# Kept first-layer products in two slots of a scratch tile, and the first pair's sums and scaled inputs one expert sooner

## The chip, the cores and the metric

The kernel runs on one core of one Trainium2 chip. The metric is device time in microseconds (us), the median of several executions. Each run lists its span (first to last instruction) and the mean granted TensorE clock; a profiled execution adds a page and a trace. Engines are written as in the profile: PE is TensorE, PEld its weight load, DVE VectorE, ACT ScalarE, POOL GpSimd, SP SyncE. A DMA is a transfer between memories that an engine's queue issues and that lands later (a store of this kernel was issued from 218.10 to 219.30 us, and what waited for it went on at 221.40). PSUM and SBUF are the two places in which this kernel has its tiles: TensorE writes its sums to PSUM tiles (`pO`, `pA`, `pV`), and the other tiles lie in SBUF.

## The reference, cut to what matters

Attention (4 batches, 8 heads, 768 positions, 64 wide; three heads causal, five with 4 sink keys and a window of 64) gives 3072 tokens of 512. A mixture of four experts follows, each with a hidden width of 1024:

```python
p = domain_probs / (domain_probs.sum(-1, keepdims=True) + 1e-09)
for e in range(E):
    h = np.maximum(x @ w1[e], 0.0)
    out += p[:, e:e + 1] * (h @ w2[e])
```

## The kernel before

The first four token tiles go through the experts in a plain way: three together, then the fourth alone. The other 20 tiles go in ten pairs. A pair's inputs are first scaled by the expert's probability. Experts 0 to 2 have a plain first layer; the last expert's first layer, and the whole second layer, are done as 2 x 2 blocks with seven products instead of eight (Winograd's form). The attention of later batches is interleaved with the pairs, so all engines run two kinds of work in one fixed order.

The first layer of the last expert uses two accumulators in PSUM, `x` and `y`, in turn. Three of its products have to be kept in SBUF until another product is added to them, and two of these are put into the output tile, which the second layer fills later:

```python
def winograd_layer1():
    s = moe.tile([P, 3, HN], FP32, name="s1", tag="sums", bufs=1)
    o = moe.tile([P, PT, DM], FP32, name="o1", tag="o", bufs=1)
    kept = [s.rearrange("p n x -> p (n x)")[:, 0 : HT * P], o[:, 0, :], o[:, 1, :]]
    ...
    def keep(n, ps):                      # ScalarE, line 1157
        nc.scalar.copy(out=kept[n], in_=ps)
    def add(n, ps, b):                    # VectorE, line 1163
        nc.vector.tensor_tensor(out=block(b), in0=ps, in1=kept[n], op=ALU.add)   # reshapes cut
        ...                               # ReLU: negative values become 0
    product(x, w1_part(0, 0), x_part(0, 0), True);  keep(0, x)      # TensorE, line 1147
    product(y, w1_part(1, 0), x_part(0, 1), True);  add(0, y, 0)
    product(x, t(1), x_sum(1), False);              keep(1, x)
    product(y, t(0), x_sum(0), True);               keep(2, y); minus(...)
    product(x, w1_part(0, 1), x_part(1, 0), False); add(2, x, 3)
    product(y, w1_part(1, 1), x_part(0, 1), False); add(1, y, 2)
    product(x, t(2), x_part(1, 1), False);          ...             # ReLU
```

At a pair's end the output tile is stored, half by half, on SyncE's queue (`store(0)`, `store(1)`). The transposes of the next group's keys and queries are DMAs on the same queue, issued after the fourth head of a group:

```python
if n == 3 and more and g > 1:
    transpose_rows(*more)        # three transposes of keys, three of queries
```

Before the first pair, while the fourth tile passes the experts, VectorE makes the weight sums `t(n)` and the scaled inputs of the first pair:

```python
for e in range(E):
    yield from plain_steps(3, 1, e, ...)      # fourth tile: layer 1, layer 2
    if e + 1 < E:
        last_weight_sum(e)
    if e + 1 < E:
        first_weight_sums()[e]()
    if e > 0:
        (lambda: scale_inputs(pairs[0], 0), lambda: scale_inputs(pairs[0], EW), scaled_sums)[e - 1]()
```

The fourth of `first_weight_sums()` comes even later, in the first pair.

The softmax here doesn't subtract the row's maximum and nothing guards it: scores larger than these inputs give would overflow.

## Time and profile before

| | before |
|---|---|
| median of the first 3 executions | 386.12 us (384.49 to 386.32) |
| profiled execution | 384.28 us, span 382.6 us |
| PE, PEld busy | 370.5, 311.5 us |
| DVE, ACT, POOL busy | 268.3, 230.3, 112.0 us |

Matmuls overlap in the pipeline (a group of eight is shown as 0.61 us at 218.69, but the next matmul starts 0.45 us later, at 219.14), so PE's busy time alone does not tell how much is left. The prediction takes the distance from each matmul's start to the next one's and subtracts the columns at 2.4 per ns; I call the remainder the excess. The trace shows that pace: eight matmuls of 128 columns take 0.45 us there, 56 ns each (32 of them, line 983, 1.79 us from 75.86 on, 56 ns each too), and eight of 512 columns 1.73 us (77.48 to 79.21), 216 ns each, so 384 more columns take 160 ns. A wait line reads: who waited, for whom, total us, times, longest us. "Idle" in a timeline's brackets is somewhat less than the excess, since the modelled end of the matmul before lies some 0.16 us after the time at which the next could have started.

### The profile page before, as it was taken

The numbers are of one execution on the slowest core, as the hardware profiler recorded it, in microseconds if no ns is written. First come the engines' busy times: TensorE is split into PE (matmuls) and PEld (weight loads), VectorE is DVE, ScalarE is ACT, GpSimd is POOL, SyncE is SP. The second block draws the span as 40 slices with busy tenths as digits, with TensorE's granted clock in tenths as the row PEclk, the third lists the DMA queues.
The fourth block names the chain that finished last, engine by engine and source line by source line (L and its number), as shares of the span: only waits on it lengthen the run. The fifth ranks groups of instructions, "written<-read, shape, count | busy, mean of one in ns | idle before, by whom it ended". The sixth has DMA issues, their size and how long they took to land.

```text
span 382.6 us, 9934 instructions
## 1 busy us (share of the span) xinstructions
PE 370.5 (97%) x4054; PEld 311.5 (81%) x4054; DVE 268.3 (70%) x590; ACT 230.3 (60%) x476; POOL 112.0 (29%) x152
## 2 busy tenths in 40 slices
PE   7889999999999999999999989999999999999996
PEld 4755456578898998899988978999998999998995
DVE  7735687589978678877667658967757757655560
ACT  4753567657776876665765675675665684551630
POOL 8933644775138029113800117303200000000000
PEclk9999999999999999999999999999999999999999
DMA  9999999999499969965940849965510210110001
GB/s 167 160 209 200 182 188 185 133 167 169 67 133 127 134 100 100 146 119 37 158 73 16 125 105 70 150 129 44 81 57 14 69 57 0 57 57 29 28 2 55
DMA packets 127193, 39.20 MB, mean 102 GB/s; under 512 B 116232, under 2 KB 120876, under 8 KB 127148
## 3 DMA queue, kind: packets, MB, share of 16 engines
q0 software_dynamic: 86816, 19.01, 56.7%
q1 hardware_dynamic: 38732, 19.18, 23.2%
q8 instruction: 31, 0.51, 0.6%
q10 hardware_dynamic: 1600, 0.39, 0.5%
q14 instruction: 14, 0.11, 0.1%
HBM read 44.88 MB, written 6.34 MB: 134 GB/s over the span
## 4 chain that ended last, share of the span: by engine, by line
PE 81%; DMA 8%; DVE 5%; POOL 3%; ACT 1%; issue 1%; POOLq 0%; ACTq 0%
PE pO L1229 32%; PE pA L1114 24%; PE pO L1147 7%; DMA w2sb<-in_moe_w_dram 7%; PE pO L1004 5%; PE pA L644 4%; PE pA L983 4%; PE pV L756 2%; PE pV L692 2%; DVE xs L1066 1%; POOL vS L302 1%; DVE kS L282 1%; DMA out_dram<-o 1%; ACT es L662 1%; POOL vR L296 1%
## 5 line engine op out<-in xcount | busy, mean ns | idle before, releaser
L1114 PE MATMUL pA<-xs,w1sb 128*128 128x256 f16 x960 | 119.1, 273 | 0.2 <-DVE xs L1066 0.2
L1229 PEld LDWEIGHTS <-hA 128*128 128x128 f16 x1120 | 106.5, 98 | 12.8
L1114 PEld LDWEIGHTS <-w1sb 128*128 128x128 f16 x960 | 89.8, 98 | 9.7 <-DVE xs L1066 0.4
L1123 ACT ACTIVATE hA<-pA 128x512 f16<-128x512 f32 x120 | 71.5, 598 | 36.8 <-PE pA L1114 34.9
L662 ACT ACTIVATE es<-pA 128x384 f16<-128x384 f32 (+2 forms) x122 | 59.0, 511 | 32.1 <-PE pA L644 28.0
L1229 PE MATMUL pO<-w2sb,hA 128*128 128x256 f16 x640 | 78.1, 272 | 0.0
L298 POOL DMA_DIRECT2D vS<-in_v_dram x30 | 29.6, 988 | 126.0 <-PE pV L756 116.5
L1229 PE MATMUL pO<-tsb,hA 128*128 128x256 f16 x480 | 58.9, 272 | 0.0
L1066 DVE TENSOR_TENSOR xs<-xT,pB 128x1024 f16<-128x1024 f16 (+1 forms) x52 | 49.5, 970 | 0.0
L939 DVE TENSOR_TENSOR hA<-hA 128x1024 f16<-128x1024 f16 x60 | 39.7, 686 | 0.8
L996 ACT ACTIVATE hA<-pA 128x384 f16<-128x384 f32 (+1 forms) x64 | 22.3, 386 | 20.3 <-PE pA L983 17.8
L983 PE MATMUL pA<-xT,w1sb 128*128 128x384 f16 (+1 forms) x256 | 31.7, 273 | 0.1
L1004 PE MATMUL pO<-w2sb,hA 128*128 128x512 f16 x128 | 30.5, 379 | 0.6 <-DMA w2sb<-in_moe_w_dram 0.6
L779 DVE TENSOR_TENSOR xT<-pV,rc 64x384 f16<-64x384 f32 x37 | 20.5, 555 | 14.1 <-ACT rc L784 11.8
L774 ACT ACTIVATE rc<-pV,eps 64x384 f32<-64x384 f32 x37 | 21.3, 576 | 9.1 <-PE pV L756 8.5
L983 PEld LDWEIGHTS <-w1sb 128*128 128x128 f16 x256 | 19.3, 98 | 8.4 <-issue 0.5
L1147 PE MATMUL pO<-xs,w1sb 128*128 128x128 f16 x320 | 24.4, 219 | 1.7 <-ACT o L1157 1.7
L666 DVE TENSOR_TENSOR es<-es,mS 128x384 f16<-128x384 f16 (+1 forms) x40 | 13.4, 344 | 16.1 <-ACT es L662 15.9
L644 PE MATMUL pA<-qT,kR 128*128 128x384 f16 (+2 forms) x120 | 22.9, 278 | 0.9 <-ACT qT L555 0.4
L1250 DVE TENSOR_TENSOR o<-pO,s 128x256 f32<-128x256 f32 x30 | 12.7, 423 | 14.6 <-PE pO L1229 11.8
L1147 PEld LDWEIGHTS <-w1sb 128*128 128x128 f16 x320 | 20.6, 98 | 2.5 <-issue 1.8
L1004 PEld LDWEIGHTS <-hA 128*128 128x128 f16 x128 | 11.9, 98 | 12.6 <-issue 0.9
(130 smaller groups left out, 460.9 us busy)
## 6 DMA issues: line engine op xcount, KB each, us to landing
pB<-p_rows SPq DMA_DIRECT2D x10, 512.0 KB, 3.6
out_dram<-o SPq DMA_DIRECT2D x19, 256.0 KB, 4.6
w1sb<-in_moe_w_dram POOLq DMA_DIRECT2D x8, 512.0 KB, 10.0
w2sb<-in_moe_w_dram POOLq DMA_DIRECT2D x4, 1024.0 KB, 13.2
vS<-in_v_dram POOLq DMA_DIRECT2D x30, 112.0 KB, 3.7
k_rows<-in_k_dram POOLq DMA_DIRECT2D x18, 128.0 KB, 4.4
q<-in_q_dram POOLq DMA_DIRECT2D x18, 128.0 KB, 6.2
vR<-in_v_dram POOLq DMA_DIRECT2D x24, 48.0 KB, 6.1
```

The costliest lines, as they stand in the source:

```text
L298: gp.dma_start(out=t[:, :, own_v(h)], in_=windows_of(v, b, h, c))
L644: nc.tensor.matmul(out=ps[:, o : o + nq], lhsT=key_tile(b, c, h, t), rhs=qTs[b, c][:, hp, q0 : q0 + nq], start=(n == 0 or not first), stop ...
L662: nc.scalar.activation(out=es[:, 0:cols], in_=ps[:, 0:cols], func=AF.Exp, scale=SC)
L939: nc.vector.tensor_tensor(out=out, in0=a, in1=b, op=ALU.subtract)
L983: nc.tensor.matmul(out=pss[ft][:, 0:cols_n], lhsT=w1sb[:, e * DMP + ct, ft * P : (ft + 1) * P], rhs=x[:, ct, :], start=(n == 0), stop=(n = ...
L996: nc.scalar.activation(out=hs[:, ft, :], in_=ps[:, 0:cols_n], func=AF.Relu)
L1004: nc.tensor.matmul(out=ps_o, lhsT=hs[:, ft, j * P : (j + 1) * P], rhs=w2sb[:, e * FTP + ft, :], start=(ft == 0), stop=(ft == FTP - 1),)
L1066: nc.vector.tensor_tensor(out=o, in0=xin, in1=pb.to_broadcast([P, DMP, n, P]), op=ALU.mult)
L1114: nc.tensor.matmul(out=ps[:, f * PC : (f + 1) * PC], lhsT=w1sb[:, e * DMP + ct, (f0 + f) * P : (f0 + f + 1) * P], rhs=xs[:, ct, :], start= ...
L1123: nc.scalar.activation(out=blocks[:, b0 : b0 + 2, k0 : k0 + 2, :].rearrange("p t f x -> p f t x"), in_=ps.rearrange("p (f t x) -> p f t x" ...
L1147: nc.tensor.matmul(out=ps[:, f * P : (f + 1) * P], lhsT=w[:, ct, f * P : (f + 1) * P], rhs=a[:, ct, :], start=(first and f == 0 and ct == ...
L1229: nc.tensor.matmul(out=ps, lhsT=a[:, k, :], rhs=b(k), start=(first and k == 0), stop=(k == KT - 1), skip_group_check=not first,)
```

## The change

The intent: a kept product shall not wait for the store of the pair before, and VectorE shall have less to do at the start of the first pair. The room for a larger scratch tile (4 instead of 3 slots of 256 columns) comes from the sums of the scaled inputs, which move into unused columns of the key tile.

```diff
-    early = moe.tile([P, XS + 2 * KH * P], FP16, name="early", tag="xs", bufs=1)
+    early = moe.tile([P, XS], FP16, name="early", tag="xs", bufs=1)
...
     def x_sum(n):
-        x = xs_of[0][:, XS + n * KH * P : XS + (n + 1) * KH * P]
-        return x.rearrange("p (c x) -> p c x", c=KH)
+
+        n0 = WT * NSH * P + n * KH * P
+        return kSf[:, n0 : n0 + KH * P].rearrange("p (c x) -> p c x", c=KH)
...
-            s = moe.tile([P, 3, HN], FP32, name="s1", tag="sums", bufs=1)
-            o = moe.tile([P, PT, DM], FP32, name="o1", tag="o", bufs=1)
-            kept = [
-                s.rearrange("p n x -> p (n x)")[:, 0 : HT * P], o[:, 0, :], o[:, 1, :]
-            ]
+            s = moe.tile([P, 4 * HN], FP32, name="s1", tag="sums", bufs=1)
+            kept = [s[:, (n % 2) * HT * P : (n % 2 + 1) * HT * P] for n in range(3)]
...
-            sums += [first_weight_sums()[3], lambda: last_weight_sum(E - 1)]
+            sums.append(lambda: last_weight_sum(E - 1))
...
+        sums = first_weight_sums()
         for e in range(E):
             n0 = (e % 2) * FTP * P
-            yield from plain_steps(3, 1, e, lambda: xT[1][:, :, 0:P], n0)
+            for n, step in enumerate(plain_steps(3, 1, e, lambda: xT[1][:, :, 0:P], n0)):
+                yield step
+                if n == FTP - 1:
+                    sums[e]()
             if e + 1 < E:
                 last_weight_sum(e)
-            if e + 1 < E:
-                first_weight_sums()[e]()
-            if e > 0:
                 (
                     lambda: scale_inputs(pairs[0], 0),
                     lambda: scale_inputs(pairs[0], EW),
                     scaled_sums,
-                )[e - 1]()
+                )[e]()
```

(The second layer's scratch tile takes the same 4 slots.)

More of the change, by code (lines that the diff above doesn't have):

```diff
@@ L1057, in scale_inputs @@
         if xs_of[0] is None:
-            xs_of[0] = moe.tile([P, XS + 2 * KH * P], FP16, name="xs", tag="xs", bufs=1)
+            xs_of[0] = moe.tile([P, XS], FP16, name="xs", tag="xs", bufs=1)
         xs = scaled(e)
@@ L1222, in pair_steps @@
         o = moe.tile([P, PT, DM], FP32, name="o", bufs=1)
-        s = moe.tile([P, 3, HN], FP32, name="s", tag="sums", bufs=1)
+        s = moe.tile([P, 4 * HN], FP32, name="s", tag="sums", bufs=1)
+        s = s.rearrange("p (n x) -> p n x", n=4)
         x = pO.tile([P, DM], FP32, name="pO", bufs=2)[:, 0:HN]
```

## The prediction

> **What bounds the kernel now.** I read the page first, then the list of waits for TensorE and for ScalarE, then the chain of waits and the timeline around the two places found there.
>
> ```profile
> span 382.6 us, 9934 instructions
> PE 370.5 (97%) x4054; PEld 311.5 (81%) x4054; DVE 268.3 (70%) x590; ACT 230.3 (60%) x476; POOL 112.0 (29%) x152
> ```
>
> TensorE is nearly always at work and the granted clock is full in all 40 slices, so the kernel is bound by TensorE. A change that removes no matmul can only remove the stalls of TensorE. The list of what TensorE waited for is short, and most of its entries lie in the first 75 us, which the change does not touch. Two entries belong to the first layer of the seven-product expert (line 1147), which the change is about; a third line tells what held ScalarE (columns: total us, times, longest us):
>
> ```profile
> PE pO L1147 <- ACT o L1157: 1.7, 1, 1.7
> ...
> PE pO L1147 <- DVE hA L1163: 0.9, 1, 0.9
> ```
>
> ```profile
> ACT o L1157 <- DMA out_dram<-o: 3.2, 1, 3.2
> ```
>
> Each happened once in ten pairs of token tiles. I took every start-to-start distance on TensorE and subtracted columns/2.4 ns. After 75 us only three excesses are above 0.2 us: 1.10 us ending at 99.35, 0.40 us ending at 158.30 and 1.84 us ending at 222.03. The rest is evenly spread, about 0.3 us in each 10 us. The last pair, which runs alone, goes from 353.46 to 379.3 us, and its 96 x 109 + 56 x 56 + 112 x 109 ns make 25.8 us: no room there.
>
> The stall at 222 us, from the timeline (start, duration, what; idle time before it and its end in brackets):
>
> ```profile
> 210.23 3.85 SPq L255 DMA_TRANSPOSE kT<-k_rows  x3
> ...
> 214.17 3.83 SPq L255 DMA_TRANSPOSE qT<-q  x3
> ...
> 218.10 1.20 SPq L1257 DMA_DIRECT2D out_dram<-o  x1
> ...
> 221.40 0.59 ACT L1157 COPY o<-pO 128x512 f32<-128x512 f32 x1 [3.23 <-DMA out_dram<-o]
> 221.88 0.60 ACT L1123 ACTIVATE hA<-pA 128x512 f16<-128x512 f32 x1
> 222.03 0.61 PE L1147 MATMUL pO<-xs,w1sb 128*128 128x128 f16 x8 [1.68 <-ACT o L1157]
> ```
>
> The second copy of a kept product goes into the output tile, of which there is one. It must not be overwritten before the previous pair's second store has read it. That store was ready after its copy at 211.71 + 0.37 = 212.08, but SyncE's queue had six transposes to issue first, so it was issued at 218.10 and landed about 221.3. The copy at 221.40 frees the accumulator that the fifth product needs, and TensorE stood still for it.
>
> The stall at 99 us is in the first pair, and the chain there runs back through VectorE without a break:
>
> ```profile
> 93.88 0.21 DVE xs L1078
> 94.10 0.02 issue
> 94.12 0.49 DVE xs L939 x2
> 94.61 1.14 DVE xs L1066
> 95.75 0.60 DVE w1sb L939
> ...
> 96.94 0.68 DVE w2sb L939
> ...
> 98.61 0.69 DVE hA L1163
> 99.31 0.04 issue
> 99.35 0.61 PE pO L1147 x8
> ```
>
> The add at 98.61 reads the second product (ended about 96.0) and frees its accumulator. It was late only because VectorE had older work to finish.
>
> [...] 97% busy hides the two stalls, and start distances show them. [...] the store's issue took 1.20 us, and what waited for it went on 3.23 us after its start. [...] the ReLU at 221.88 had its products since about 220.2 and stood behind the blocked copy. [...] Here eight of 128 columns take 218.69 to 219.14, 56 ns each, and eight of 256 columns 0.87 us, 109 ns each[...].
>
> **The change, part by part.** The order of instructions of both builds shows the same number on each engine; nothing is added or removed, so the busy sums stay. Three things move.
>
> 1. The kept products go to two slots of the scratch tile. In the built program the second kept copy of pairs 2 to 10 waits for two DMA semaphores before, and for none after. Its new condition is that slot 0 has been read before the third copy writes it. That reader is the add that the fourth product already waited for (same accumulator), so no new wait arises. Gain: at 222.03 TensorE would have gone on at about 220.19, so 1.84 us. In the other eight pairs ScalarE did not wait for a store, so the gain there is 0.
>
> 2. The sums of the scaled inputs move to the unused tail of the key tile (columns 4480 to 4992 of 5120; the later heads' windows use only the first 4480). The copies into that tile get no new wait in the build. Time: 0. It pays for the larger scratch tile, no more.
>
> 3. In the first pair, VectorE's work moves ahead of 91 us: three sums of the inputs and the fourth weight sum leave the queue ahead of the add at 98.61. Start to start these are 0.32 (93.80 to 94.12), 0.41 (94.12 to 94.53) and 0.60 us (95.67 to 96.27), 1.33 us in all. The add then starts at 98.61 - 1.33 = 97.28, and TensorE may go on at 99.35 - 1.33 = 98.02. TensorE was done with its earlier work at 98.14 + 0.11 = 98.25 (the last of eight 256-column matmuls from 97.38). So the wait goes, with 0.2 us to spare: 1.10 us.
>
> What part 3 costs: the same work now stands between 79 and 90 us. There I walked VectorE's new order by hand with the old durations (0.67 for a draining add, 0.60 for a weight sum, 1.14 for scaling). The first weight sum takes the place ahead of the drain at 79.41, which slips to about 80.0; the 1.53 us of idle time before the drain at 82.92 takes in the first scaling, and that drain slips to about 83.2; then weight sum 0.60, scaling 1.14, weight sum 0.60 bring the copy of the keys from 85.93 to about 86.2. The first score matmul that needs those keys started at 86.46, when the copies ended at 86.44; now they end at about 86.7. The drains have a second accumulator behind them and are not needed for over 3 us, so they hold nothing up; the key copy can cost up to 0.25 us, I take 0.15.
>
> Sum: -1.84 - 1.10 + 0.15 = -2.8 us of 382.6, a span of 379.8, or 0.73%.
>
> **Rivals.** (a) The stall at 222 is replaced: TensorE, 1.8 us earlier, finds the adds, keys or queries not ready. For it: the transposes of the next queries are issued until 218.1 at fixed pace, whatever TensorE does. Against: no score matmul of the next group runs within the next 7 us shown, the adds of this pair were waiting for TensorE (16.3 us of waits of line 1163 for it), and all other large transfers are released by TensorE's own progress. It would keep the time at about 385. (b) The early work on VectorE costs more than it gives: the key copy or a drain slips by a microsecond, or the scaled probabilities are not there at 81.5 us. The broadcast of them was issued at 69.58 and takes 3.6 us (the median), so they are there. If the key copy slips by 1 us, the time is about 384.3. (c) The unprofiled runs, median 386.12 against 384.28 us for the profiled one, lose their extra 1.8 us to a longer wait for that same store, since a late store is what varies between executions. Then the gain is up to 4.6 us, 381.5. Nothing in the profile tells this from a slower start, where w2 and v loads hold the chain for 26 us.
>
> **Range and chances.** 386.12 x (379.8 / 382.6) = 383.3. The runs before spread over 1.83 us, so the median carries about 0.9 us of noise, and the gain itself is between 1 and 4.6 us: 381.5 to 385.3. Two per cent is 7.7 us, over twice the stalls that the change can reach, so faster by 2% is nearly excluded; a loss of 2% would need a new wait repeated in most pairs, and the build shows no such new condition.
>
> **What would show it.** Right: no wait of ScalarE for a store, no TensorE start excess above 0.3 us in the first layer of pairs 1 and 5, the late store still behind six transposes but with nobody waiting, busy sums within 1 us, a small wait of TensorE for the key copy near 86.6. Part 3 is wrong if the add of the first pair still ends after its accumulator is wanted; part 1 if another wait of similar size stands within some microseconds after 220. The whole is wrong if a wait appears in every pair, or if excess grows in the first 75 us, where both kernels have the same order.

## The result, and the profile after

| | before | after |
|---|---|---|
| median of 6 executions each | 385.59 us (384.49 to 386.40) | 381.57 us (381.28 to 383.13) |
| ratio | | 0.9906 (95%: 0.9879 to 0.9933) |
| span of the profiled execution | 382.6 us | 380.0 us |

A ratio is the mean time of one kernel's fast runs over that of the other's in the same rounds, so it is not quite the ratio of the two medians. The interval lies below 1, so the gain of about 0.9% is real. The predicted 383.3 us is 1.7 us too high, and the measured median lies just inside the lower end of the range.

The head of the page after:

```profile
span 380.0 us, 9930 instructions
PE 370.4 (97%) x4054; PEld 311.5 (82%) x4054; DVE 267.9 (70%) x590; ACT 230.3 (61%) x476; POOL 110.8 (29%) x152
```

TensorE's work and its share are as before, while the span is 2.6 us shorter: work was not removed, gaps were. The list of TensorE's waits after (who, for whom, us, times, longest) has no line left of the last expert's first layer, which is now line 1145:

```profile
PE pO L756 <- DMA vS<-in_v_dram: 1.7, 1, 1.7
...
PE pA L1115 <- DVE xs L1066: 0.2, 1, 0.2
```

The first line is the start of the kernel, where TensorE waits for the values of one head; this line will be needed below. In the list of ScalarE's waits no line names a store. The timeline where the late store was (start, duration, what):

```profile
213.53 3.85 SPq L255 DMA_TRANSPOSE qT<-q  x3
...
217.42 0.58 ACT L1155 COPY s<-pO 128x512 f32<-128x512 f32 x1
...
217.47 1.27 SPq L1256 DMA_DIRECT2D out_dram<-o  x1
...
219.55 0.61 PE L1145 MATMUL pO<-xs,w1sb 128*128 128x128 f16 x8
```

The store is as late as it was, behind the same transposes. But the second kept copy now writes the scratch tile; it starts at 217.42, before the store is even issued, and the fifth product at 219.55 waits for nothing. In the first pair the timeline after reads:

```profile
86.25 0.76 DVE L266 COPY kR<-kT 64x768 f16<-64x768 f16 x2
...
86.90 0.39 PE L644 MATMUL pA<-qT,kR 128*128 128x128 f16 x2
...
97.73 0.68 DVE L1161 TENSOR_TENSOR hA<-pO,s 128x512 f16<-128x512 f32 x1
...
98.69 0.61 PE L1145 MATMUL pO<-kS,t1sb 128*128 128x128 f16 x8
```

The add that frees the second accumulator ends at 98.41, and the fourth product needs it at 98.69. Before, the add came after TensorE had been ready for a microsecond.

To compare executions I cut each trace at one fixed place: the first matmul of the fourth tile's first second layer (line 1004). It starts at 77.48 us before and 77.80 us after. From there to the end it takes 305.10 us before and 302.20 us after, so the part that the change touches gained 2.90 us in these two executions, and 0.32 us was lost ahead of it, where both kernels issue the same matmuls.

### The profile page after: what moved, and what is told of

It is laid out like the page before. It is cut to its first block, busy times and chain, and to the rows that moved or that the text cites.

```text
span 380.0 us, 9930 instructions
## 1 busy us (share of the span) xinstructions
PE 370.4 (97%) x4054; PEld 311.5 (82%) x4054; DVE 267.9 (70%) x590; ACT 230.3 (61%) x476; POOL 110.8 (29%) x152
## 4 chain that ended last, share of the span: by engine, by line
PE 85%; DMA 7%; POOL 3%; DVE 3%; ACT 1%; issue 0%; POOLq 0%
PE pO L1228 32%; PE pA L1115 27%; PE pO L1145 8%; DMA w2sb<-in_moe_w_dram 7%; PE pO L1004 6%; PE pA L644 5%; PE pA L983 4%; PE pV L756 2%; PE pV L692 2%; POOL vS L302 1%; DVE xs L1066 1%; POOL vR L296 1%; ACT es L662 1%; DVE kS L282 0%; POOL early L441 0%
## 5 line engine op out<-in xcount | busy, mean ns | idle before, releaser
L1115 PEld LDWEIGHTS <-w1sb 128*128 128x128 f16 x960 | 89.7, 98 | 9.8 <-DVE xs L1066 0.4
L1161 DVE TENSOR_TENSOR hA<-pO,s 128x512 f16<-128x512 f32 x30 | 20.6, 687 | 17.2 <-PE pO L1145 16.3
L983 PEld LDWEIGHTS <-w1sb 128*128 128x128 f16 x256 | 19.3, 98 | 8.4 <-issue 0.5
## 6 DMA issues: line engine op xcount, KB each, us to landing
vS<-in_v_dram POOLq DMA_DIRECT2D x30, 112.0 KB, 3.7
```

Of the source, the lines that this page charges most:

```text
L983: nc.tensor.matmul(out=pss[ft][:, 0:cols_n], lhsT=w1sb[:, e * DMP + ct, ft * P : (ft + 1) * P], rhs=x[:, ct, :], start=(n == 0), stop=(n = ...
L1115: nc.tensor.matmul(out=ps[:, f * PC : (f + 1) * PC], lhsT=w1sb[:, e * DMP + ct, (f0 + f) * P : (f0 + f + 1) * P], rhs=xs[:, ct, :], start= ...
```

## The experiments

Every kernel gave correct results. "Tail" below is the time from that cut to the end of the trace; the two stalls are TensorE's excess in the first pair (near 99 us) and in the fifth pair (near 222 us).

| kernel | median, us | ratio to before (95%) | cut, us | tail, us | stall 1 | stall 2 | half clock from |
|---|---|---|---|---|---|---|---|
| before, first trace | 385.59 | | 77.5 | 305.1 | 1.10 | 1.84 | |
| before, second trace | 386.64 (1 run) | | 77.6 | 307.3 | 1.10 | 2.42 | 223.9 |
| after, first trace | 381.57 | 0.9906 (0.9879 to 0.9933) | 77.8 | 302.2 | none | none | |
| after, second trace | 382.66 | 0.9924 (0.9896 to 0.9952) | 78.8 | 302.3 | none | none | 21.8 |
| two slots alone | 383.25 | 0.9940 (0.9916 to 0.9965) | 77.5 | 303.2 | 1.10 | none | |
| earlier sums alone | 383.85 | 0.9959 (0.9931 to 0.9987) | 78.9 | 304.1 | none | 1.92 | 21.5 |
| transposes behind the store | 382.97 | 0.9935 (0.9909 to 0.9961) | 78.9 | 303.2 | 1.10 | none | 21.4 |
| fourth weight sum alone | 384.99 | 1.0000 (0.9944 to 1.0056) | 77.7 | 304.5 | 0.49 | 1.87 | |
| input sums' place alone | 385.89 (1 run) | | 78.9 | 305.2 | 1.09 | 1.95 | 21.7 |
| before, one more store | 387.10 | 1.0029 (1.0004 to 1.0053) | 79.0 | 306.0 | 1.10 | 2.51 | 21.2 |
| after, one more store | 382.14 | 0.9900 (0.9870 to 0.9929) | 80.0 | 302.0 | none | none | 22.0 |
| after, second expert's inputs sooner | 382.12 | 0.9896 (0.9860 to 0.9932) | 78.0 | 301.6 | none | none | |
| after, values first | 382.44 | 0.9913 (0.9878 to 0.9949) | 78.3 | 302.1 | none | none | |
| after, inputs sooner, more warming | 381.12 | 0.9891 (0.9856 to 0.9926) | 77.8 | 301.6 | none | none | |

The kernel before in the same rounds had medians of 385.16 us (first four experiments), 386.40, 386.25 and 385.74 us. In the last of these rounds one execution of it was slow (432.3 us, clock 0.849) and is left out of the ratio.

### Two slots alone

The diff's parts for the kept products and the sums' place, without those of the first pair.

```diff
-            kept = [s[...][:, 0 : HT * P], o[:, 0, :], o[:, 1, :]]
+            kept = [s[:, (n % 2) * HT * P : (n % 2 + 1) * HT * P] for n in range(3)]
     # and x_sum in the key tile, as in the change; shortened here
```

> Only the kept products in two slots (with the sums of the inputs in the key tile's tail, which makes the room); VectorE's order in the first pair as before. My theory, two independent stalls: ScalarE waits for no store, TensorE's excess near 222 us (1.84 us) is gone, the excess near 99 us (1.10 us) is still there with 1.0 to 1.2 us; the span of the profile falls by 1.8 us. Rival A, one stall hides the other: less than 1 us. Rival B, the store wait is longer in unprofiled executions: the mean time falls by 2.8 us or more (ratio 0.993 or less). Without B the ratio is about 0.995.

Measured: the stall near 222 us is gone, the one near 99 us is whole. The list of TensorE's waits still has the first pair's line (its line number is 1144 here):

```profile
PE pO L1144 <- DVE hA L1160: 0.9, 1, 0.9
```

The tail is 303.19 us, 1.91 us less than the first trace of before, against 1.84 predicted. The times fell by 0.60%, 2.3 us, which is between the two outcomes (about 0.5% without a longer store wait in unprofiled runs, 0.7% or more with it).

### Earlier sums alone

```diff
-            sums += [first_weight_sums()[3], lambda: last_weight_sum(E - 1)]
+            sums.append(lambda: last_weight_sum(E - 1))
     # and the loop over the experts of the fourth tile, as in the change
```

> Only the weight sums and the first pair's inputs one expert sooner; the kept products stay in the output tile. Two independent stalls: the excess near 99 us is gone, the store stall near 221 us is still there with 1.5 to 2.1 us, the span falls by about 1.1 us less the wait for the key copy (0 to 0.25 us); ratio about 0.997. Rival A, one stall hides the other: the store stall grows by what was won at 99 us, since the six transposes before the store are issued at their own pace, and the time stays as before. Rival B: ratio 0.997 too, and the spread of the times stays as wide as before.

Measured: the stall near 99 us is gone, and the store's is there, hardly longer:

```profile
PE pO L1147 <- ACT o L1157: 1.8, 1, 1.8
```

The tail is 304.10 us, 1.00 us less than before (1.10 less up to 0.25 predicted). Together the two parts gain 1.91 + 1.00 = 2.91 us, and the whole change 2.90: the two stalls add up, within the 0.3 us by which tails of one order of work differ, and Rival A is out.

### The same store stall removed in another way

Here the buffers stay as before. Only the six transposes of one group are put into SyncE's queue one head later.

```diff
-                if n == 3 and more and g > 1:
+                if n == (4 if g == 5 else 3) and more and g > 1:
```

> The kernel before, kept products in the output tile, with one thing moved: the six transposes ahead of the late store of the fifth pair are put into SyncE's queue one head later, behind the store. If the queue order makes the stall, the store is issued about 212 us instead of 218, ScalarE's 3.2 us wait and TensorE's 1.84 us near 222 us are gone, and the gain is as of the two slots (span -1.8 us, ratio about 0.995), without any change of buffers. If the store is late for another reason (slow landing, bandwidth), the wait stays above 1 us. A cost would show as a new wait of TensorE for keys or queries of the next group near 238 us.

SyncE's timeline of this kernel (x2 is both stores of the pair):

```profile
211.29 2.60 SPq L1257 DMA_DIRECT2D out_dram<-o  x2
...
216.82 4.43 SPq L255 DMA_TRANSPOSE kT<-k_rows  x3
221.34 3.84 SPq L255 DMA_TRANSPOSE qT<-q  x3
```

The two stores now stand ahead of the six transposes and are issued between 211.29 and 213.89, and the stall is gone: tail 303.23 us, 1.87 us less, the same as with two slots. So the stall needed both halves: the shared tile, and a queue that issued six transposes first. The transposes came some 5 us later than before (counted from the cut) and no wait for keys or queries appeared, so these had at least that much slack. One execution of six was slow (388.6 us) and is left out of the ratio.

### The fourth weight sum alone

```diff
+                if e == E - 1 and n == FTP - 1:
+                    first_weight_sums()[3]()          # in the fourth tile's last expert
-            sums += [first_weight_sums()[3], lambda: last_weight_sum(E - 1)]
+            sums.append(lambda: last_weight_sum(E - 1))
```

> The kernel before with only the fourth weight sum (0.60 us on VectorE) taken out of the first pair's queue and done one expert's layer sooner. If the stall near 99 us is a queue of VectorE's work, as I say, it shrinks by just this: from 1.10 to 0.50 us (0.4 to 0.6). If the add waits for something else (the copy of the kept product, a semaphore of a store), the stall stays at 1.1 us or goes entirely. The stall near 222 us stays at 1.8 us. From the first expert's second layer of the fourth tile to the end: 305.1 - 0.6 = 304.5 us in the profile; the ratio, 0.998, lies inside the noise.

The waits of TensorE:

```profile
PE pO L1147 <- ACT o L1157: 1.7, 1, 1.7
...
PE pO L1147 <- DVE hA L1163: 0.3, 1, 0.3
```

The excess went from 1.10 to 0.49 us, by 0.61, for 0.60 us of work taken out of the queue. The tail is 304.53 us, 0.57 less. So stall 1 is a queue of older VectorE work, and it shrinks one for one. The ratio can't show it.

### The input sums' place alone

```diff
-        x = xs_of[0][:, XS + n * KH * P : XS + (n + 1) * KH * P]
+        n0 = WT * NSH * P + n * KH * P
+        # ... of kSf
```

> The kernel before with only the sums of the scaled inputs moved to the key tile's unused columns. No wait and no duration should change: both stalls as before (1.1 and 1.8 us; 2.4 and half a clock if the store lands late), 305.1 us from the fourth tile's first second layer to the end without a halved clock. A false dependence on the key tile would show as waits of the copies of keys for the sums, 0.3 us or more in each group.

Tail 305.22 us, both stalls present (1.09 and 1.95 us). In this trace the part neither gains nor costs; it makes room.

### The change again, and the kernel before again

> The changed kernel again, for a second trace and more times. The profiles told of 2.6 us of span, the medians of 4.0 us. If the difference is chance (which execution was profiled), the mean gain of this series lies between 2.6 and 4.0 us and the spread of both kernels is alike, about 1.9 us. If the store wait is what varies (Rival B), the changed kernel's times lie closer together than those of the kernel before. In the trace: no excess above 0.4 us on TensorE after 75 us, as in the first trace.

The second trace after has a tail of 302.34 us, 0.14 more than the first; it has 0.24 us of excess at the copy of keys (near 88 us), where the first trace has 0.12. The mean time in this series is 382.55 us against 385.45 for before, 2.9 us. The spread did not shrink (2.45 us, against 2.88 of eleven executions before), so at this point the store wait was not what made the times vary. The page of this trace showed what might: the granted clock dips in the third slice of 40.

> The kernel before, a second trace. What varies between executions lies in the first 79 us (the start of the fourth tile's first second layer came between 77.5 and 78.9 us in six traces), and the rest is fixed: 305.1 us from there to the end in the first trace, 305.0 to 305.3 here, with the two stalls of 1.1 and 1.8 us. If the store wait is what varies, the second stall differs by more than 0.3 us from 1.84.

I was wrong here. The tail is 307.29 us, not 305.1 to 305.3. In the page's row of the granted clock one slice is not full:

```profile
PEclk9999999999999999999999989999999999999999
```

Stretches of the trace around the store stall of this second trace show it in full (stretch in us, its length, busy us and instructions of PE, PEld, DVE, ACT, POOL, granted clock, DMA share, GB/s):

```profile
core 0: us, PE busy (x) PEld busy (x) DVE busy (x) ACT busy (x) POOL busy (x), PEclk, DMA share, GB/s
...
220.44:223.85 3.41, 1.15 (x18) 1.01 (x14) 0.00 (x0) 1.70 (x4) 0.00 (x0) 1.00 0.87 245
223.85:227.26 3.41, 3.41 (x28) 2.76 (x27) 2.56 (x6) 2.42 (x5) 0.98 (x1) 0.50 0.07 28
```

Two stretches of the same length around the store stall in the first trace of before:

```profile
219.73:223.14 3.41, 1.73 (x27) 1.54 (x25) 0.00 (x0) 1.74 (x4) 0.00 (x0) 1.00 0.59 200
223.14:226.55 3.41, 3.41 (x47) 3.13 (x45) 2.60 (x6) 3.33 (x8) 0.98 (x1) 1.00 0.33 75
```

In the second trace ScalarE waited 3.8 us for the store instead of 3.2, the stall was 2.42 us instead of 1.84, and then TensorE ran at half clock for 3.41 us: 28 matmuls in the next stretch instead of 47. Half a clock for 3.41 us costs 1.7 us, an estimate from that stretch. So in this trace the tail has a second price, which came behind a store stall that was a little longer: 305.1 + 0.6 + 1.7 = 307.4 us, against 307.3 measured.

In six other traces half clock begins at 21.2 to 22.0 us (last column of the table), after TensorE's wait for the values of one head. The lists of TensorE's waits give this wait as 2.0, 2.0, 2.0, 2.3 and 3.3 us in five of the six (earlier sums alone, transposes behind the store, the second trace after, before and after with one more store), and as 0.6 to 1.7 us in six traces without half clock there. So at both places that the prediction could not tell apart, "slow start" and "longer store wait", half clock was recorded after a wait of TensorE. What sets the clock is not shown.

### Making the stall longer on purpose

```diff
         else:
+            if nt0 == 10:
+                store(0)          # the same bytes to the same rows again
             store(1)
```

Done to both kernels.

> The kernel before, made worse: ahead of the late store of pair 4 the first store of that pair is issued a second time (the same bytes to the same rows), which costs SyncE's queue one more issue of about 1.2 us. Theory of the clock, from the second trace of the kernel before (a stall of 2.26 us there was followed by 3.41 us at half clock, one of 1.68 us in the first trace was not): the stall of TensorE becomes 2.9 to 3.2 us instead of 1.84, a stretch of 3.41 us at half clock follows within some microseconds, and from the fourth tile's first second layer to the end it takes 305.1 + 1.2 + 1.7 = 308.0 us; the mean granted clock of all timed executions is 0.996 or less. Rival: the halved clock there was chance; then 306.3 us and clocks of 1.0 in over half of the executions.

> The changed kernel with the same additional store at the same place. The kept products no longer wait for a store, so nobody waits for the later one: 302.2 to 302.5 us from the fourth tile's first second layer to the end, ratio to the kernel before as of the change (0.990 to 0.993), no stall near 220 us, no half clock there. If the store is still in someone's way (the first add into the output tile near 229 us), a new wait of VectorE or TensorE appears there.

In the kernel before, the additional issue cost less than I had assumed: the two stores together took 1.70 us to issue instead of one store's 1.20, and the stall became 2.51 us, not 3. In the profiled execution no half clock followed. The stretch of that length with most of the stall, and the one after it (columns as above):

```profile
222.56:225.98 3.42, 1.44 (x21) 1.34 (x21) 0.00 (x0) 2.08 (x5) 0.00 (x0) 1.00 0.74 241
225.98:229.39 3.41, 3.41 (x47) 3.12 (x45) 2.94 (x6) 3.33 (x7) 0.98 (x1) 1.00 0.50 40
```

The stall began before the first of these stretches, and TensorE was busy for 1.44 us of it, against 1.15 us in the second trace of before and 1.73 in the first; half clock came after the 1.15 alone. The tail was 305.98 us, 0.88 more than before: 0.67 of stall and 0.29 at the key copy, and no halved clock after the stall. The theory's sum for this trace (308.0) was wrong in its stall and in its certainty: a stall of 2.51 us had no half clock behind it and one of 2.42 us had, so the stall's length alone does not tell, and what else it takes is not shown. In the timed executions all six clocks were 0.994 to 0.996 (the profiled one lost its share near 21 us), against seven of eleven of the kernel before in the same rounds. Unprofiled executions don't tell where the share was lost, and six of six against seven of eleven can be chance. In the changed kernel the additional store did nothing: tail 302.01 us, no wait for it, clocks below 0.998 in two of six.

Fast executions with a mean clock of 0.997 or less, over all calls from the second on (a stretch like that of the second trace of before, 3.41 us at half clock, is 3.41 / 2 / 381 = 0.45%):

| | executions | with a lowered clock |
|---|---|---|
| kernel before (both idle places) | 43 | 22 |
| after (all three series), two slots, transposes behind the store, inputs sooner (only the start's) | 35 | 10 |

The third series of after is the one with one more store. The first series of after is counted, the first of before gave no clocks. Two kernels that also keep both idle places stand in neither row, earlier sums alone and the fourth weight sum alone; they had 2 of 10. With them it is 24 of 53 against 10 of 35, and a difference of that size comes by chance in about one case of eight (22 of 43 against 10 of 35: one of sixteen; Fisher's exact test). So the table leans the way the theory says, and does not prove it. In the series of the first four experiments, the executions of before with a lowered clock have a mean of 386.44 us (4) and the others 384.88 us (7), 1.55 us apart; in the three later rounds the two means are 1.66, 1.79 and 0.89 us apart.

### Two attempts to go further

> The changed kernel and, for every later pair, the second expert's inputs scaled at the end of the pair before (behind the scaling for the last expert) instead of at the pair's start. Aimed at what is left of the same kind: 0.40 us near 158 us, where TensorE waits for this scaling behind the copies of keys. If VectorE has room there, that excess goes and the rest of the trace from the fourth tile on falls from 302.3 to 301.9 us. Rival: the scaling delays the copies of keys or the last adds by 1.2 us and makes a new wait of TensorE of the same size in some pair; then 302.3 us or more. The ratio to the kernel before, 0.99 to 0.993, cannot tell these apart; the trace can.

The edit: in a pair's second layer `scale_inputs(nxt, 1)` follows `scale_inputs(nxt, EW)`, and the call at the next pair's start is left to the first pair. The excess near 158 us is gone and no new one came; the tail is 301.59 us, 0.4 to 0.8 us less than in the four traces with the change's order there (302.0, 302.1, 302.2, 302.3; the last two have 0.12 and 0.24 us at the key copy). The times can't show it.

> The changed kernel, with the values of the last two heads of the first group loaded before the first expert's weights instead of behind them. Aimed at the largest stall that both kernels have, 1.7 to 2.1 us near 21 us, TensorE waiting for these values, in the stretch whose length varies. If the values alone are late, that stall shrinks to below 0.5 us and the fourth tile's first second layer starts 1 us or more sooner (77.5 instead of 77.8 to 78.8 us at the least). Rival: the loading of weights sets this stretch (the chain has 26 us of the second layer's weights), and the time comes back as a wait for weights between 25 and 47 us; then no gain.

```diff
-    load_v(0, 0, [2, 1, 3, 4, 6])
+    load_v(0, 0, [2, 1, 3, 4, 6, 5, 7])
     load_w1(0, 0, F)
-    load_v(0, 0, [5, 7])
```

The wait for the values went, and the wait for the second layer's weights grew from 0.6 us (first trace after) to 2.0 us:

```profile
PE pO L1003 <- DMA w2sb<-in_moe_w_dram: 2.0, 1, 2.0
```

The rival holds: the cut comes at 78.3 us, inside the range of the others (77.5 to 80.0), so nothing was won. That the stretch is set by the loading of weights as a whole fits this one trace, but is not shown further.

> The changed kernel with the earlier scaling of the second expert's inputs, and six more of the warming matmuls (256 columns, 109 ns each, 0.65 us in all) in front of the fifth head's values, where TensorE idles 0.6 to 3.3 us waiting for them. [...] Theory: [...] the mean clock is 0.999 or more in five of six executions, 301.6 us from the fourth tile's first second layer to the end as with the earlier scaling alone, ratio to the kernel before 0.986 to 0.990. Rival: the additional matmuls delay the start by their 0.65 us, or clocks of 0.994 to 0.996 stay as frequent (a third); then no gain over the earlier scaling alone, ratio 0.990 or more.

```diff
-                warm_up(ps, {3: 4, 4: 4, 5: 6, 7: 10}.get(h, 0), 256)
+                warm_up(ps, {3: 4, 4: 4, 5: 12, 7: 10}.get(h, 0), 256)
     # and the inputs of the second expert sooner, as above
```

The six additional matmuls fill time in which TensorE only waits: the cut comes at 77.8 us, against 78.0 us without them. All six executions had a clock of 0.999 or 1.0, and five of the six lie between 381.05 and 381.26 us. The median, 381.12 us, is the lowest of all kernels here, against 385.74 us for before in the same rounds; the ratio, 0.9891, lies in the expected range, and its interval overlaps that of the change. Whether it beats the change in time can't be told from these rounds. Its tail, 301.59 us, is that of the inputs sooner alone. That the additional matmuls keep the clock up is not shown: at a rate of 10 in 35, six executions without a lowered clock come by chance in about 13% of cases.

## Why the prediction was right or wrong

**The bound.** Right: PE's busy time is the same within 0.1 us, and the gain is gaps. One reading goes further than the trace: that the store landed about 221.3. ScalarE's copy went on at 221.40, 3.30 us after the store's start at 218.10 (3.23 us is the length of ScalarE's wait), so it was let go 2.10 us after the 1.20 us of the issue; when the data had arrived is not shown. The predicted agreement of busy sums within 1 us fails for POOL alone (112.0 to 110.8 us), which decides nothing here.

**Part 1, two slots, 1.84 us.** Right in mechanism and size where the clock stays full: the tail shortens by 1.91 us with this part alone, and by 1.87 us when the transposes are moved instead. Both halves of the cause, tile and queue order, are shown.

**Part 2, the sums' place, 0.** Right: tail 305.22 against 305.10 us.

**Part 3, 1.10 us less 0.15 for the key copy.** Right: 1.00 us alone. The step "0.60 us off the queue is 0.60 us off the stall" is shown by the fourth sum alone (0.61). The add had 0.28 us to spare, 0.2 was predicted. The excess at the key copy was 0.12 and 0.24 us in the two traces of after, but below 0.03 us in the five other traces with the earlier sums, and 0.29 us in one trace without them (before, one more store). So it is of the predicted size where it came, but I can't put it down to the change.

**The sum, 2.8 us.** In the trace the touched part gained 2.90 and 2.76 us in the two traces, against the first trace of before. The times gained more: 3.6 us in the mean of the first series (385.48 to 381.88), 2.9 in the second. The term that was mis-sized is "386.12 x (379.8 / 382.6) = 383.3", 1.7 us above the measured 381.57. About 0.5 us of that is its base: the median of before was 386.12 us in three executions and 385.59 in six. For the rest, it took one profiled execution for the typical one.

Five traces keep the store stall as it was: 1.84, 1.87, 1.92, 1.95 and 2.42 us. Their mean is 0.16 us above the predicted 1.84, and one of the five had a halved clock after it, an estimate of 1.7 / 5 = 0.3 us in the mean. Rival (c) had the direction right, a longer wait for the same store in other executions, but not the larger part of its price: in the trace that showed it, 0.6 us of longer wait came with 1.7 us of half clock.

The clocks of the timed executions give the same size: a stretch of 3.41 us at half clock less in 17 to 23% of executions (24 of 53, or 22 of 43, against 10 of 35), an estimate of 0.3 to 0.4 us, if that difference is real. So about 3.3 us (2.8 to 2.9 in the traces, 0.16 and 0.3) would be expected, and the two series gave 3.6 and 2.9; what is left is within the spread of single executions (1.9 us before and after) and stays unexplained. That the first median lies in the predicted range by 0.07 us is luck in the last step; the median of the second series, 382.66 us, lies well inside.

**Rivals (a) and (b).** Both fell: no wait replaced the store's (also not with transposes 5 us later), and what could be put down to the work moved ahead of 91 us is 0.24 us at most.

## What to carry to other kernels

A buffer shared between a store and an early write of the next round ties an engine to a DMA queue's order; look at what is queued ahead of the store, since here either a place of its own or another order freed it, for the same gain (1.91 and 1.87 us). The late store's own issue took 1.20 us behind the six transposes (1.27 in the first trace after), against 0.33 to 0.39 us for the five other stores that the first trace of before shows singly. Where one engine is nearly always busy, list start-to-start excesses instead of busy shares: after 75 us, three entries (1.10, 0.40 and 1.84 us) held nearly all that was won. A stall can come with more than its length: in the one trace that shows it at the store, 0.6 us of longer stall came with another 1.7 us of half clock. Filling such a wait with idle matmuls is worth a trial, but its gain in time is not shown here.
